# Strided attention in 36-token tiles, loads of k on GpSimd, and weight slots at multiples of 128 bytes, in a sparse attention and MoE kernel

## The chip, the cores and the metric

The kernel runs on one core of one Trainium2 chip. The metric is the device time of one execution in microseconds. The core has five engines with queues of their own: TensorE (PE in the profile; its weight loads are PEld), VectorE (DVE), ScalarE (ACT), GpSimd (POOL) and SyncE (SP), which here issues DMAs. Two on-chip memories are used: a large one in which tiles and weights lie, and eight accumulation banks of 128 x 512 fp32 that PE writes.

## The reference

Attention over 4 batches, 8 heads, 576 tokens and a head dimension of 64, then two feed-forward layers over all 2304 tokens (`_moe_ref` and `_moe2_ref`):

```
rel = pos[:, None] - pos[None, :]
mask_local = (rel >= 0) & (rel < 32)
mask_strided = (rel >= 0) & (pos[None, :] % 32 == pos[:, None] % 32)
# heads 0-3 local, heads 4-7 strided
scores = where(mask, scale * q @ k.T, -1e9)
scores = scores - max(scores)
attn = exp(scores) / (sum(exp(scores)) + 1e-9)
x = (attn @ v)                       # to (2304, 512)
h = x @ w_in                         # w_in 512 x 2048
x = (h * tanh(softplus(h))) @ w_out  # w_out 2048 x 512
h = max(max(x @ w1, x @ w2), x @ w3) # 512 x 768 each
out = h @ w_out2                     # 768 x 512
```

## The kernel before, in words

*Attention.* A head pair is two heads side by side in the 128 partitions. Pairs 0 and 1 of a batch are local, pairs 2 and 3 strided. In a strided head, token t sees only earlier tokens with the same residue t mod 32, of which there are 18. The tokens are taken by residue, 3 residues (54 tokens) to a tile, so that a head has 11 tiles, the last with 2 residues (36 tokens). A unit of work (`unit`, L377) is up to four tiles of a head pair. It computes scores (L413, two matmuls a tile, one per head), on DVE the scaled mask (L426) and the row maximum (L432), on ACT one exponential for each tile with the row's sum accumulated (L438), on DVE guard, reciprocal and normalisation (L445, L448, L451), one PE transpose a tile (L458), on ACT its copy out of the bank (L463), the products with v (L471), and the result's high part on ACT (L489) and low part on DVE (L493). One accumulation bank holds all of a unit, from its scores to its result. Numbers are split into a high and a low part and three partial products are added (`PASSES`), which is why x and the weights have two parts. A plain fp32 matmul (scores, products with v) leaves two records in the trace.

*Loads.* q and k of batch 0 come early in long rows and are transposed by PE (L355). Those of batches 1 to 3 come as four DMAs each for a head pair (`load_qk`, L801), with runs of 32 numbers, and are transposed by DVE (L329). There are two raw buffers for q and two for k. v of a strided pair comes in six DMAs (L834), of a local one in three (L820, L826). All these DMAs and those of the weights (L787, L790) are issued by SP in one order, so a later one stands behind an earlier one that still waits for its buffer.

*Feed-forward layers.* Weights come in 56 pieces of 128 x 512, each as two words a number, and are converted by ACT and DVE (L253 to L281) into slots: 5 of pool a, later 11 of pool x where the attention's buffers were, and 8 of pool y on the right side of the memory where `hr` was. The first four pieces of w_in are applied in blocks of 288 tokens while attention is still running (L516, copied by L526), their products with w_out in blocks of 512 tokens start after it (L543). Then come the other twelve pieces (L516, L543), and the second layer (L590, L615). The last block has 256 tokens.

*Order.* A planner (`Plan`) sets one order for all engines before anything is emitted. It gives every step a cost on its engine, simulates the engines, and always takes the ready step of the lowest rank. Where it expects PE to wait until the first product of L543, it writes matmuls of 256 columns on zeros (`fill`, L839) that take up the expected time. Ring buffers (`RING`) and banks are reused in turn, and a step waits for the last reader of what it writes.

Of the kernel before, what the change touches and what calls it, by code (L numbers as in the profile page):

```python
# [10 lines left out]
F32 = mybir.dt.float32  # L11
# [23 lines left out]
RES = 3  # L35
ATT_BANKS = ("a0", "a1", "a2", "acc1", "acc2")
RAW_BANKS = ("h0", "acc3")
# [152 lines left out]
def build_plan(k, B, H, S, D, DM, FF, FF2, wide):  # L190
# [110 lines left out]
    unit_tiles = {True: ((0, 1, 2), (3, 4, 5), (6, 7, 8)), False: ((0, 1, 2, 3), (4, 5, 6, 7), (8, 9, 10))}  # L301
    per_batch = 3 * H // 2
# [8 lines left out]
    def attention():  # L311
        n = 0
        for i, (b, hp) in enumerate(pairs):
# [7 lines left out]
            for nm in ("q", "k") if b else ():  # L321
                for g in range(4):
                    add("qk_load", "sp", S * PACKET[128], (lambda g=g, nm=nm, b=b, hp=hp, r=r: k.load_qk(nm, g, b, hp, k.raw(nm, r))),
                        writes=[("raw", nm, r, g)], rank=lr)

                def tr(nm=nm, r=r, local=local):
                    t = k.qkT(nm, r)
                    tv = t.rearrange("p (j r) -> p j r", r=STRIDE) if local else t.rearrange("p (r j) -> p j r", j=NJ)
                    nc.vector.transpose(out=tv, in_=k.raw(nm, r))  # L329

                add("tr", "dve", 669, tr, reads=[("raw", nm, r, g) for g in range(4)], writes=[("qT", nm, r)], rank=rk0 - 0.5)
            vparts = k.v_parts(hp)
            for j in range(vparts):
                v_cost = PACKET[256] * (LK * (2 if j == 0 else NL - 1) if local else NJ * (NS - (j % RES == RES - 1)))
                add("v_load", "sp", v_cost, (lambda j=j, b=b, hp=hp, rv=rv: k.load_v(j, b, hp, k.v(rv))),
                    writes=[("v", rv, j_) for j_ in range(j, 2 * RES, vparts)], rank=lr + 0.5)
            for u, tiles in enumerate(unit_tiles[local]):
                unit(n, i, u, tiles, b, hp, local, r, rv)
                n += 1
            if i == H // 2 - 1:  # L340
                add("hrpool", "dve", 0, k.open_hrpool, writes=[("earlypool",)], rank=-1)

    def early_qk(i, b, hp, local, r, rk0, lr):
# [5 lines left out]
        for j in range(2):  # L349
            for nm in ("q", "k"):  # L350
# [9 lines left out]
                def copy(nm=nm, j=j, tag=tag):  # L360
# [3 lines left out]
                    else:  # L364
                        t = t.rearrange("p (r j) -> p r j", j=NJ)[:, :, NJ // 2 * j:NJ // 2 * (j + 1)]
                        src = src.rearrange("p (j r) -> p r j", r=STRIDE)
# [10 lines left out]
    def unit(n, i, u, tiles, b, hp, local, r, rv):  # L377
# [5 lines left out]
        tag = ATT_BANKS[n % len(ATT_BANKS)]  # L383
        bk = ("bank", tag)
# [24 lines left out]
        for j, tl in enumerate(tiles):  # L409
            def scores(j=j, tl=tl):  # L410
                kw = LK if local else width(tl)
                for h in range(2):
                    nc.tensor.matmul(  # L413
                        ps()[LQ * h:LQ * h + width(tl), j * K:j * K + kw],
                        lhsT=cols("q", h, tl), rhs=cols("k", h, tl), start=True, stop=True,
                    )
            add("scores", "pe", 212 if local else 142, scores, reads=[("qT", "q", r), ("qT", "k", r)], writes=[bk], rank=rk, cols=4 * (K if local else width(tl)))

        def mask():
# [4 lines left out]
            else:  # L424
                m = k.m_first[:, 1, :].unsqueeze(1).broadcast_to([rows, nt, K])
            nc.vector.scalar_tensor_tensor(  # L426
                out=sv(), in0=ps()[:rows, :nt * K].rearrange("p (n c) -> p n c", c=K),
# [6 lines left out]
        add("mask", "dve", dve(nt * K), mask, reads=[bk], writes=[sb, *sk], rank=rk)  # L434
# [456 lines left out]
```

## Time and profile before

| | |
|---|---|
| time, three runs | 807.07, 807.09, 807.59 us (median 807.09) |
| the profiled execution | 807.78 us, of it a span of 806.0 us |
| PE busy | 797.0 us (99%), 5017 records |
| DVE busy | 360.7 us (45%) |
| ACT busy | 320.9 us (40%) |
| POOL busy | 4.4 us (1%) |
| PE's granted clock | 1.00 over the whole span |
| share of the span in the chain that ended last | PE 92%, DMA 3%, ACT 2%, DVE 2% |

The span goes from the first to the last instruction of the profiled execution. Busy times of different engines lie beside each other. The chain is followed back from the last instruction, at each step to what released it. The attention with the first blocks of 288 tokens takes the first 154 us or so, and everything after that is matmuls of 512 columns and their small work on DVE and ACT.

### The profile page before, as it was taken

The numbers are of one execution on the slowest core, as the hardware profiler recorded it, in microseconds if no ns is written. First come the engines' busy times: TensorE is split into PE (matmuls) and PEld (weight loads), VectorE is DVE, ScalarE is ACT, GpSimd is POOL, SyncE is SP. The second block draws the span as 40 slices with busy tenths as digits, with TensorE's granted clock in tenths as the row PEclk, the third lists the DMA queues.
The fourth block names the chain that finished last, engine by engine and source line by source line (L and its number), as shares of the span: only waits on it lengthen the run. The fifth ranks groups of instructions, "written<-read, shape, count | busy, mean of one in ns | idle before, by whom it ended". The sixth has DMA issues, their size and how long they took to land.

```text
span 806.0 us, 12605 instructions
## 1 busy us (share of the span) xinstructions
PE 797.0 (99%) x5017; PEld 669.3 (83%) x5017; DVE 360.7 (45%) x769; ACT 320.9 (40%) x839; POOL 4.4 (1%) x22
## 2 busy tenths in 40 slices
PE   9999999999999999999999999999999999999998
PEld 7878888988888888888888899888888888888897
DVE  6988886895931311311321179981212211122222
ACT  5978878997732322312322257630110110110111
POOL 2000000000000000000000000000000000000000
PEclk9999999999999999999999999999999999999999
DMA  9877750944900100100010079200100010010010
GB/s 206 157 152 132 135 102 22 349 148 170 326 0 1 53 0 1 53 0 1 1 52 0 1 227 322 105 1 0 53 1 0 16 38 1 0 53 1 0 53 27
DMA packets 119690, 59.66 MB, mean 74 GB/s; under 512 B 91984, under 2 KB 110416, under 8 KB 119632
## 3 DMA queue, kind: packets, MB, share of 16 engines
q1 hardware_dynamic: 118448, 58.57, 26.5%
q8 instruction: 39, 0.64, 0.3%
q10 hardware_dynamic: 1184, 0.30, 0.2%
q14 instruction: 19, 0.16, 0.1%
HBM read 49.41 MB, written 9.44 MB: 73 GB/s over the span
## 4 chain that ended last, share of the span: by engine, by line
PE 92%; DMA 3%; ACT 2%; DVE 2%; issue 1%; SPq 0%; DVEq 0%; ACTq 0%
PE bank_acc L543 24%; PE bank_a L590 21%; PE bank_a L516 13%; PE bank_acc L615 9%; PE bank_h L516 7%; PE bank_h L590 7%; PE bank_acc L516 3%; PE bank_a L413 2%; PE bank_a L471 1%; DMA wslot<-in_moe_w_dram 1%; PE bank_a L458 1%; DMA wslot<-in_moe_w_out_dram 1%; PE bank_acc L413 1%; ACT s L438 1%; PE bank_acc L471 1%; PE bank_acc L458 1%
## 5 line engine op out<-in xcount | busy, mean ns | idle before, releaser
L543 PE MATMUL bank_acc<-g,wslot 128*128 128x512 f32 (+1 forms) x960 | 205.4, 370 | 1.4 <-ACT g L537 1.0
L543 PEld LDWEIGHTS bank_acc<-g,wslot 128*128 128x128 f32 x960 | 168.3, 188 | 33.7 <-ACT g L537 1.2
L590 PE MATMUL bank_a<-x,wslot 128*128 128x512 f32 (+1 forms) x816 | 174.7, 369 | 0.0
L590 PEld LDWEIGHTS bank_a<-x,wslot 128*128 128x128 f32 x816 | 142.3, 188 | 26.9
L538 DVE TENSOR_TENSOR g<-h,g 128x512 fp32r<-128x512 f32 (+1 forms) x80 | 51.1, 639 | 194.8 <-ACT g L537 194.8
L516 PE MATMUL bank_a<-x,wslot 128*128 128x512 f32 (+1 forms) x540 | 117.2, 369 | 0.0
L516 PEld LDWEIGHTS bank_a<-x,wslot 128*128 128x128 f32 x540 | 94.5, 188 | 17.9
L599 DVE TENSOR_TENSOR h<-bank_a,h 128x512 f32<-128x512 f32 (+1 forms) x46 | 29.2, 635 | 138.9 <-PE bank_a L590 138.9
L615 PE MATMUL bank_acc<-wslot,g 128*128 128x512 f32 x324 | 78.8, 391 | 0.0
L516 PE MATMUL bank_h<-x,wslot 128*128 128x288 f32 (+2 forms) x372 | 74.5, 339 | 0.0
L615 PEld LDWEIGHTS bank_acc<-wslot,g 128*128 128x128 f32 x324 | 60.5, 188 | 12.8
L535 ACT ACTIVATE h<-bank_a 128x512 f32<-128x512 f32 (+1 forms) x45 | 25.0, 555 | 109.8 <-PE bank_a L516 109.8
L516 PEld LDWEIGHTS bank_h<-x,wslot 128*128 128x128 f32 x372 | 58.5, 188 | 7.4
L601 ACT ACTIVATE g<-h 128x512 fp32r<-128x512 f32 (+1 forms) x30 | 17.7, 589 | 116.1 <-DVE h L599 116.1
L590 PE MATMUL bank_h<-x,wslot 128*128 128x512 f32 (+1 forms) x264 | 58.8, 371 | 0.0
L438 ACT ACTIVATE s<-s,st 118x54 f32<-118x54 f32 (+1 forms) x160 | 55.5, 352 | 7.2 <-DVE st L432 6.9
L590 PEld LDWEIGHTS bank_h<-x,wslot 128*128 128x128 f32 x264 | 46.7, 188 | 9.0
L537 ACT CAST g<-h 128x512 fp32r<-128x512 f32 (+1 forms) x80 | 46.3, 579 | 4.5 <-PE bank_acc L543 2.7
L253 ACT ACTIVATE wt<-wslot 128x512 f32<-128x512 f32 x56 | 37.9, 678 | 22.7 <-DVE wslot L281 9.7
L277 ACT CAST wslot<-wt 128x512 fp32r<-128x512 f32 x56 | 34.5, 621 | 15.3 <-DVE wt L267 15.1
L281 DVE TENSOR_TENSOR wslot<-wt,wslot 128x512 fp32r<-128x512 f32 x56 | 38.6, 692 | 3.4 <-ACT wslot L277 3.4
L596 ACT COPY h<-bank_a 128x512 f32<-128x512 f32 (+1 forms) x22 | 12.0, 548 | 69.8 <-PE bank_a L590 69.8
(71 smaller groups left out, 680.4 us busy)
## 6 DMA issues: line engine op xcount, KB each, us to landing
wslot<-in_moe_w_out_dram SPq DMA_DIRECT2D x22, 512.0 KB
wslot<-in_moe_w_dram SPq DMA_DIRECT2D x18, 512.0 KB
wslot<-in_moe_w_in_dram SPq DMA_DIRECT2D x16, 512.0 KB
out_dram<-wt SPq DMA_DIRECT2D x18, 256.0 KB
x2p<-ev SPq DMA_DIRECT2D x16, 256.0 KB
ev<-x2p SPq DMA_DIRECT2D x16, 256.0 KB
rawq<-in_q_dram SPq DMA_DIRECT2D x48, 72.0 KB
rawk<-in_k_dram SPq DMA_DIRECT2D x48, 72.0 KB
```

The lines of the kernel that those rows point to most:

```text
L253: nc.scalar.mul(k.wt(r2).bitcast(F32), k.words(slot)[1].bitcast(F32), 2.0 ** -111)
L277: nc.scalar.copy(out=k.open_slot(slot)[:, 0, :], in_=k.wt(r2).bitcast(F32))
L281: nc.vector.tensor_tensor(out=s[:, 1, :], in0=k.wt(r2).bitcast(F32), in1=s[:, 0, :], op=ALU.subtract)
L438: nc.scalar.activation(sv()[:, j, :], sv()[:, j, :], AF.Exp, bias=mx()[:, j:j + 1], accum_out=dn()[:, j:j + 1],)
L516: nc.tensor.matmul(k.bank(hb)[:, :n], lhsT=wap(("in", f), a, c), rhs=k.x[:, q, c, t0:t0 + n], start=(c == 0 and m == 0), stop=(c == KC - 1 ...
L535: add(name, "act", act(n, psum=not stored), lambda: nc.scalar.activation(Hh(), src(), AF.Mish, scale=W_SCALE), reads=sread, writes=[HK], r ...
L537: add("gh", "act", act(n), lambda: nc.scalar.copy(out=g()[:, 0, :n], in_=Hh()), reads=[HK], writes=[G0], rank=s)
L538: add("gl", "dve", dve(n), lambda: nc.vector.tensor_tensor(out=g()[:, 1, :n], in0=Hh(), in1=g()[:, 0, :n], op=ALU.subtract), reads=[HK, G0 ...
L543: nc.tensor.matmul(k.bank(f"acc{c}")[:, :n], lhsT=wap(("out", f), a, c), rhs=g()[:, q, :n], start=(first and m == 0), stop=(last and m == 2),)
L590: nc.tensor.matmul(k.bank(hb)[:, :n], lhsT=wap((w_, f), a, c), rhs=k.x[:, q, c, t0:t0 + n], start=(c == 0 and m == 0), stop=(c == KC - 1 a ...
L599: add("m2", "dve", dve(n), (lambda hb=hb: nc.vector.tensor_tensor(out=m_(), in0=k.bank(hb)[:, :n], in1=m_(), op=ALU.max)), reads=[("bank", ...
L615: nc.tensor.matmul(k.bank(ab)[:], lhsT=k.g(rg)[:, a, c * P:(c + 1) * P], rhs=t[:, q, :], start=(f == 0 and m == 0), stop=(f == F2C - 1 and ...
```

## The change

- A strided tile has 2 residues (36 tokens), so a head has 16 tiles. They are taken in two units of four steps; a step handles two tiles of a head pair, residues 2n and 2n+1 (tile n) and 16 more than these (tile n + 8; `par` 0 and 1), with both heads: four matmuls of scores of 36 x 36, in two banks, that lie in the four quadrants of 64 x 64 of the array. The products with v do likewise. One PE transpose of 100 x 100 takes two tiles. A new function `pair_unit` emits such a unit; `unit` keeps the local ones.
- Its softmax has one row maximum, one subtraction, one exponential, one sum and one normalisation for eight tiles; the subtraction and the sum are DVE's, the exponential has no bias and no accumulator.
- Local units take one bank for scores (a0, a1 in turn) and another for transposes and results (a2, acc1, acc2 in turn); a strided unit has two for scores and two for the rest.
- Tokens of a strided pair stand in another order inside a tile, and v of a strided pair comes in four DMAs of 36 rows of 2 KB.
- The DMAs of k for batches 1 to 3 are issued by GpSimd. GpSimd also clears the five buffers s (now 128 x 512) at the start, behind the masks.
- The pad `edge` is 24 numbers (96 bytes a partition) in place of 8 (32 bytes). The tiles that lie on the right side behind it, the eight slots of pool y among them, move from 64 past a multiple of 128 bytes to a multiple.

```diff
-RES = 3
+RES = 2
+ATT_PAIRS = (("a0", "a1"), ("a2", "acc1"))
+IN_BANKS, OUT_BANKS = ATT_BANKS[:2], ATT_BANKS[2:]
...
-    unit_tiles = {True: ((0, 1, 2), (3, 4, 5), (6, 7, 8)), False: ((0, 1, 2, 3), (4, 5, 6, 7), (8, 9, 10))}
+    unit_tiles = {True: ((0, 1, 2), (3, 4, 5), (6, 7, 8)), False: ((0, 1, 2, 3), (4, 5, 6, 7))}
...
-                    add("qk_load", "sp", S * PACKET[128], (lambda ...: k.load_qk(nm, g, b, hp, k.raw(nm, r))),
+                    add("qk_load", "sp" if nm == "q" else "qa", S * PACKET[128], (lambda ...: k.load_qk(nm, g, b, hp, k.raw(nm, r))),
...
-        tag = ATT_BANKS[n % len(ATT_BANKS)]
+        tin, tag = IN_BANKS[n % len(IN_BANKS)], OUT_BANKS[n % len(OUT_BANKS)]
...
+    def pair_unit(n, i, u, tiles, b, hp, local, r, rv):
...
+        for j, tl in enumerate(tiles):
+            for par in range(2):
+                def scores(j=j, tl=tl, par=par):
+                    for h in range(2):
+                        o = LQ * (h ^ par)
+                        nc.tensor.matmul(
+                            k.bank(ins[par])[o:o + K, j * K:(j + 1) * K],
+                            lhsT=qk("q", h, NS // 2 * par + tl), rhs=qk("k", h, NS // 2 * par + tl), start=True, stop=True,
+                        )
+                add("scores", "pe", 38, scores, reads=[("qT", "q", r), ("qT", "k", r)], writes=[ik[par]], rank=rk, cols=2 * K)
...
+        add("rowmax", "dve", dve(2 * nt * K), lambda: nc.vector.tensor_reduce(out=mx(), in_=sv(), axis=AX.X, op=ALU.max, negate=True),
+            reads=[sb], writes=[mk], rank=rk)
+        add("sub", "dve", dve(2 * nt * K), lambda: nc.vector.tensor_tensor(out=sv(), in0=sv(), in1=many(mx()), op=ALU.add),
+            reads=[mk], writes=[sb], rank=rk)
+        add("exps", "act", act(2 * nt * K), lambda: nc.scalar.activation(sv(), sv(), AF.Exp), writes=[sb], rank=rk)
+        add("sum", "dve", dve(2 * nt * K), lambda: nc.vector.tensor_reduce(out=dn(), in_=sv(), axis=AX.X, op=ALU.add),
+            reads=[sb], writes=[dk], rank=rk)
...
+                nc.tensor.transpose(
+                    k.bank(outs[0])[:rows, j * P:j * P + rows], k.buf(sb)[:rows, j * P:j * P + rows], k.ident[:rows, :rows]
+                )
...
+                    for h in range(2):
+                        c = j * P + LQ * (h ^ par)
+                        nc.tensor.matmul(
+                            k.bank(outs[par])[D * h:D * (h + 1), j * K:(j + 1) * K],
+                            lhsT=k.v(rv)[o:o + K, h, tl, :], rhs=k.buf(pb)[o:o + K, c:c + K], start=True, stop=True,
+                        )
...
-    upper.tile([P, 8], F32, name="edge")
+    upper.tile([P, 24], F32, name="edge")
...
-        nc.sync.dma_start(
+        (nc.sync if nm == "q" else nc.gpsimd).dma_start(
...
-            h, r = divmod(j, RES)
-            vr = v[b, 2 * hp + h].rearrange("(j r) d -> j r d", r=STRIDE)
-            n = len(range(r, STRIDE, RES))
-            nc.sync.dma_start(out=t[NJ * r:NJ * (r + 1), h, :n, :], in_=vr[:, r::RES, :])
+            h, par = divmod(j, 2)
+            n = NS // 2 * D
+            o = LQ * par
+            nc.sync.dma_start(
+                out=t[o:o + RES * NJ, h, :NS // 2, :].rearrange("p n d -> p (n d)"),
+                in_=v[b, 2 * hp + h].rearrange("(p n) d -> p (n d)", n=NS)[:, n * par:n * (par + 1)],
+            )
...
+        for t in s_t:
+            nc.gpsimd.memset(t[:], 0.0)
```

The lines of the program move by 7 to 104 with it: the fillers L839 become L938, the first layer's L516 and L543 become L612 and L639, the second layer's L590 and L615 become L686 and L711, the loads of q and k L801 become L897, those of strided v L834 become L930.

The planner writes another order for every engine. On PE, batch 0's first strided units stand in these rows before (s is the masked scores, pt their transpose, earlyq and earlyk the early loads, a row ends with its count):

```order
L839 MATMUL bank_acc_105<-x 128x256 x7
L471 MATMUL bank_a_101<-pt_124,v_134 64x64 x6
L458 MATMUL bank_a_102<-ident,s_110 54x118 x4
L839 MATMUL bank_acc_105<-x 128x256 x7
L355 MATMUL bank_h_104<-ident,earlyq_96 128x96 x3
L355 MATMUL bank_acc_108<-ident,earlyk_97 128x96 x3
L458 MATMUL bank_a_103<-ident,s_111 54x118 x4
L839 MATMUL bank_acc_105<-x 128x256 x3
L471 MATMUL bank_a_102<-pt_122,v_135 64x54 x8
```

and now in these (L528 scores, L556 transposes, L569 products with v, L481 the same of a local unit):

```order
L365 MATMUL bank_acc_108<-ident,earlyk_97 128x96 x3
L938 MATMUL bank_acc_105<-x 128x256 x30
L556 MATMUL bank_a_103<-ident,s_110 100x100 x4
L938 MATMUL bank_acc_105<-x 128x256 x5
L365 MATMUL bank_h_104<-ident,earlyq_96 128x96 x3
L569 MATMUL bank_a_103<-pt_122,v_135 64x36 x8
L569 MATMUL bank_acc_106<-pt_122,v_135 64x36 x8
L938 MATMUL bank_acc_105<-x 128x256 x3
L365 MATMUL bank_h_104<-ident,earlyq_96 128x96 x3
```

Between the scores of the first strided unit and its transposes stand fillers in one run of 30, and there are more of them around its products with v; the unit's products go to two banks. Up to the end of batch 0 there are 53 fillers before and 134 now, and over the whole program 61 and 155.

On SP, the loads that follow batch 0's stand in these rows before:

```order
L787 DMA wslot<-in_moe_w_out_dram 128x1024
L801 DMA rawq_125<-in_q_dram 32x18x32 x4
L801 DMA rawk_127<-in_k_dram 32x18x32 x4
L801 DMA rawq_126<-in_q_dram 32x18x32 x4
L801 DMA rawk_128<-in_k_dram 32x18x32 x4
L801 DMA rawq_125<-in_q_dram 32x18x32 x4
L801 DMA rawk_127<-in_k_dram 32x18x32 x3
L834 DMA v_133<-in_v_dram 18x11x64 x2
L834 DMA v_133<-in_v_dram 18x10x64
L834 DMA v_133<-in_v_dram 18x11x64 x2
L834 DMA v_133<-in_v_dram 18x10x64
```

On SP they stand in these now, without k, and with four DMAs for each strided v:

```order
L922 DMA v_134<-in_v_dram 96x8x64 x2
L897 DMA rawq_125<-in_q_dram 32x18x32 x4
L897 DMA rawq_126<-in_q_dram 32x18x32 x4
L897 DMA rawq_125<-in_q_dram 32x18x32 x4
L930 DMA v_133<-in_v_dram 36x512 x4
L897 DMA rawq_126<-in_q_dram 32x18x32 x4
L930 DMA v_134<-in_v_dram 36x512 x4
```

On POOL k's loads now follow the five cleared buffers:

```order
L960 MEMSET s_112 128x512
L960 MEMSET s_113 128x512
L897 DMA rawk_127<-in_k_dram 32x18x32 x4
L897 DMA rawk_128<-in_k_dram 32x18x32 x4
L897 DMA rawk_127<-in_k_dram 32x18x32 x4
```

SP's rows of the whole program go from 182 to 142, the DMAs of k leave between those of q, and POOL has 48 of them.

## Rows read from the trace of the kernel before

**Rows 1.** The page's busy times: busy us (share of the span) x instructions.

```profile
PE 797.0 (99%) x5017; PEld 669.3 (83%) x5017; DVE 360.7 (45%) x769; ACT 320.9 (40%) x839; POOL 4.4 (1%) x22
```

**Rows 2.** Busy us (x instructions) by stretch; then clock, DMA share, GB/s.

```profile
10.00:41.70 31.70, 31.56 (x477) 26.19 (x473) 30.15 (x98) 28.92 (x126) 0.00 (x0) 1.00 0.96 190
41.70:60.00 18.30, 16.60 (x193) 13.21 (x190) 15.81 (x43) 13.00 (x52) 0.00 (x0) 1.00 0.76 141
60.00:100.00 40.00, 40.00 (x579) 33.52 (x579) 34.45 (x107) 32.85 (x145) 0.00 (x0) 1.00 0.74 134
100.00:140.00 40.00, 39.90 (x526) 33.98 (x525) 30.77 (x92) 31.38 (x134) 0.00 (x0) 1.00 0.33 65
...
153.90:460.00 306.10, 306.10 (x1363) 252.32 (x1362) 108.87 (x184) 117.22 (x206) 0.00 (x0) 1.00 0.18 62
```

**Rows 3.** Timeline, 48 to 50 us: start, us, instruction, [idle before, releaser].

```profile
48.04 0.68 ACT L253 ACTIVATE wt<-wslot 128x512 f32<-128x512 f32 x1 [2.32 <-DMA wslot<-in_moe_w_out_dram]
...
49.99 0.53 PE L516 MATMUL bank_acc<-x,wslot 128*128 128x288 f32 x2 [1.00 <-ACT wslot L277]
```

**Rows 4.** Timeline of PE, 143 to 154 us.

```profile
143.40 1.10 PE L839 MATMUL bank_acc<-x 128*128 128x256 f32 x8
144.34 1.74 PE L516 MATMUL bank_h<-x,wslot 128*128 128x288 f32 x12
...
153.91 2.45 PE L543 MATMUL bank_acc<-g,wslot 128*128 128x512 f32 x10
```

**Rows 5.** Timeline of PE, 63 to 72 us, strided units.

```profile
63.17 0.61 PE L413 MATMUL bank_a<-qTk,qTq 64*54 64x54 f32 x16
63.70 0.59 PE L458 MATMUL bank_acc<-ident,s 118*54 118x118 f32 x4
64.06 1.05 PE L516 MATMUL bank_h<-x,wslot 128*128 128x288 f32 x6
...
69.88 0.25 PE L471 MATMUL bank_a<-pt,v 36*64 36x36 f32 x2
69.89 0.26 PE L413 MATMUL bank_acc<-qTk,qTq 64*36 64x36 f32 x2
69.95 0.23 PE L471 MATMUL bank_a<-pt,v 36*64 36x36 f32 x2
...
71.30 0.67 PE L471 MATMUL bank_a<-pt,v 54*64 54x54 f32 x16
71.90 0.67 PE L516 MATMUL bank_acc<-x,wslot 128*128 128x288 f32 x3
```

**Rows 6.** Groups of DVE by shape, 0 to 160 us: busy us, mean ns.

```profile
L432 DVE TENSOR_REDUCE st<-s 128x3 f32<-128x288 f32 x24 | 10.5, 437 | 0.1
...
L432 DVE TENSOR_REDUCE st<-s 118x4 f32<-118x216 f32 x16 | 6.0, 373 | 0.1
...
L493 DVE TENSOR_TENSOR x<-bank_a,x 128x216 fp32r<-128x216 f32 x10 | 5.4, 545 | 3.9 <-ACT x L489 3.7
...
L493 DVE TENSOR_TENSOR x<-bank_a,x 128x144 fp32r<-128x144 f32 x5 | 2.1, 415 | 0.0
```

**Rows 7.** Timeline of SP and DVE, 78 to 86 us.

```profile
78.33 1.23 DVE L329 STREAM_TRANSPOSE qTq<-rawq 128x576 f32<-128x576 f32 x1
...
85.75 2.06 SPq L801 DMA_DIRECT2D rawk<-in_k_dram  x4
...
85.88 1.25 DVE L329 STREAM_TRANSPOSE qTq<-rawq 128x576 f32<-128x576 f32 x1
```

**Rows 8.** Timeline of PE in the second layer, 572 to 603 us.

```profile
572.90 2.88 PE L590 MATMUL bank_a<-x,wslot 128*128 128x512 f32 x12
575.62 0.62 PE L615 MATMUL bank_acc<-wslot,g 128*128 128x512 f32 x2
...
600.10 2.96 PE L590 MATMUL bank_h<-x,wslot 128*128 128x512 f32 x12
602.90 5.76 PE L590 MATMUL bank_a<-x,wslot 128*128 128x512 f32 x24
```

More of the change, by code (lines that the diff above doesn't have):

```diff
@@ L327, in tr @@
                     t = k.qkT(nm, r)
-                    tv = t.rearrange("p (j r) -> p j r", r=STRIDE) if local else t.rearrange("p (r j) -> p j r", j=NJ)
-                    nc.vector.transpose(out=tv, in_=k.raw(nm, r))
+                    src = k.raw(nm, r)
+                    if local:
+                        t = t.rearrange("p (j r) -> p j r", r=STRIDE)
+                    else:
+                        t = in_tile(t, nm).rearrange("p n a j -> p j a n")
+                    nc.vector.transpose(out=t, in_=src)
                 add("tr", "dve", 669, tr, reads=[("raw", nm, r, g) for g in range(4)], writes=[("qT", nm, r)], rank=rk0 - 0.5)
-            vparts = k.v_parts(hp)
+            vparts = 3 if local else 4
             for j in range(vparts):
-                v_cost = PACKET[256] * (LK * (2 if j == 0 else NL - 1) if local else NJ * (NS - (j % RES == RES - 1)))
+                v_cost = PACKET[256] * LK * (2 if j == 0 else NL - 1) if local else 300
                 add("v_load", "sp", v_cost, (lambda j=j, b=b, hp=hp, rv=rv: k.load_v(j, b, hp, k.v(rv))),
-                    writes=[("v", rv, j_) for j_ in range(j, 2 * RES, vparts)], rank=lr + 0.5)
+                    writes=[("v", rv, j_) for j_ in range(j, VKEYS, vparts)], rank=lr + 0.5)
             for u, tiles in enumerate(unit_tiles[local]):
-                unit(n, i, u, tiles, b, hp, local, r, rv)
+                (unit if local else pair_unit)(n, i, u, tiles, b, hp, local, r, rv)
                 n += 1
@@ L413, in scores @@
                     nc.tensor.matmul(
[L414 removed]
+                        k.bank(tin)[LQ * h:LQ * h + width(tl), j * K:j * K + kw],
                         lhsT=cols("q", h, tl), rhs=cols("k", h, tl), start=True, stop=True,
                     )
[L417 removed]
+            add("scores", "pe", 212 if local else 142, scores, reads=[("qT", "q", r), ("qT", "k", r)], writes=[ik], rank=rk, cols=4 * (K if local else width(tl)))
         def mask():
@@ L475, in av @@
                     )
-            add("av", "pe", 160, av, reads=[pk] + [("earlypool",)] * (rv >= RING["v"]) + [("v", rv, j_) for j_ in range(2 * RES)], writes=[bk], rank=rk, cols=8 * width(tl) * K / P)
+            add("av", "pe", 160, av, reads=[pk] + [("earlypool",)] * (rv >= RING["v"]) + [("v", rv, j_) for j_ in range(VKEYS)], writes=[bk], rank=rk, cols=8 * width(tl) * K / P)
         def io(part):
@@ L741, in sparse_attention_moe_kernel @@
     qT_t = {nm: many(atc, "qT", [P, S], suffix=nm) for nm in "qk"}
-    v_t = many(atc, "v", [P, 2, NS, D])
-    v_t += [early_pool.tile([P, 2, NS, D], F32, name=f"v{i}") for i in range(RING["v"], RING["v"] + 2)]
+    v_t = many(atc, "v", [P, 2, NL, D])
+    v_t += [early_pool.tile([P, 2, NL, D], F32, name=f"v{i}") for i in range(RING["v"], RING["v"] + 2)]
     m_first = atc.tile([P, 3, LK], F32, name="m_first")
```

74 lines of the change are left out of this document (64 added, 10 removed).

## The prediction

> **What bounds the kernel now.** I read first the busy time of each engine over the whole span, then the table of stretches, then single rows of the timeline. The first says that TensorE (PE) is busy 99% of 806.0 us [rows 1]: little is to be had from waits, so the time changes by what PE is given to do and by how fast it does it. The table of stretches [rows 2] tells where that is different. In batch 0's attention (10 to 41.7 us) PE is busy 31.56 of 31.70 us, but VectorE (DVE) is busy 30.15 and ScalarE (ACT) 28.92: three engines are full, and part of PE's work is filler. From 41.7 to 60 us PE has 1.70 us of idle time, the largest of the attention; the rows there show it waiting for a converted weight, and ACT waiting for that weight's DMA [rows 3]. From 60 to 140 us PE is full again and DVE is busy 65.2 of 80 us. From 153.91 us, where the first 512-column block of the second matrix starts [rows 4], to 460 us PE is never idle. [...]
>
> So the end follows PE: each microsecond of instructions added to it before 153.9 us moves the end by as much, unless PE stood waiting there, and each matmul made faster later takes as much off.
>
> **The change part by part.**
>
> *Fillers.* The planner writes matmuls of 256 columns where it expects PE to idle. The order of PE holds 61 of them before and 155 after, 94 more, 81 of them in batch 0. Eight of them take 0.94 us from the first's start to the next instruction [rows 4], 0.118 us each: 94 x 0.118 = 11.1 us. They would be free where PE waits anyway, but in batch 0 PE has only 0.14 us of idle time left. Against them stands the strided work that left the same places.
>
> *Strided attention on PE.* Now 88 tiles of up to 54 tokens, afterwards 128 of 36. A fp32 matmul leaves two records, so scores go from 352 to 512 records, and the products with v as well; transposes go from 88 to 64. Now a group of 16 score records takes 0.53 us (63.17 to 63.70), 0.033 each, 4 transposes take 0.36, 0.09 each, and 16 records with v take 0.60, 0.0375 each [rows 5]. Before: 352 x 0.033 + 352 x 0.0375 + 88 x 0.09 = 32.7 us. For the new shape the trace has the 36-wide last tile of a head: in one place two records of products with v and two of scores start within 0.07 us (69.88 to 69.95) [rows 5], 0.018 each. That is with two quadrants of the array in use; the new units go round all four, and if these ran side by side it would be half, 0.009. The cost of going from one kind of matmul to another is what separates 0.033 from the 54-wide pace; scaling 0.018 by 54/36 gives 0.027, and 16 x (0.033 - 0.027) = 0.1 us a group, so I take 0.13 a group for both kinds. After: 16 units of two groups, 32 x 0.13 = 4.2; 64 transposes x 0.09 = 5.8; and 1024 records, 18.4 us at 0.018 or 9.2 at 0.009. Together 28.4 or 19.2: between -4.3 and -13.5 us. On the other side, if four narrow matmuls gain nothing over the 54-wide rates, 512 x 0.033 + 512 x 0.0375 + 5.8 = 41.9, or +9.2. I take 0.016, near the one row of that width, because the two records of a matmul must follow each other in one quadrant: 16.4 + 4.2 + 5.8 = 26.4, **-6.3 us**.
>
> [...] The trace shows four 36-wide records starting 0.018 us apart [rows 5]. [...]
>
> *Softmax.* In place of 88 small exponentials on ACT there are 16 of 288 columns; DVE gets a subtraction and a sum that ACT had done. By DVE's rows [rows 6] a strided head pair costs now three masks, maxima and normalisations (all at the maximum's rate, 373 ns at 216 columns, about 0.32 for the short one) and three low parts (545, 545, 415): 3.2 + 1.5 = 4.7 us. Afterwards it costs four masks of 144 columns (373 less 72 columns at the 0.89 ns by which 288 columns differ from 216: 0.31), eight passes of 288 columns at 0.437 and four low parts at 0.415: 1.2 + 3.5 + 1.7 = 6.4. That is +1.7 us a pair, 3.4 in batch 0 and 10.2 in the other three. I cost it at nothing: in batch 0 the added fillers make PE's side longer by more than DVE's 3.4, and in the later batches DVE has 14.8 us free in 80 [rows 2]. If the cover is gone, it is the third case below.
>
> *Loads.* 48 of the DMAs of k leave SyncE's queue (SP) for GpSimd's, and 16 of the strided v go altogether, as each tile of v comes in 4 DMAs of long rows in place of 6. SP issues four DMAs of k in 2.06 us [rows 7], so its queue is some 48 x 0.5 = 25 us shorter, and the weights that queue behind these loads come earlier. The wait at 48 to 50 us [rows 3] should go. What stands behind it: the idle time of 41.7 to 60 us is 1.70 us in all, so **-1.7 us** at most; I take it whole, with 0 as the other end. GpSimd also clears five buffers of 512 columns at the start. Its 22 instructions take 4.4 us now [rows 1], 0.2 each, so five wider ones may take 1 to 4 us and end before 10 us, where batch 0's softmax starts: nothing, or 2 us if they don't.
>
> *Slots.* The wider pad moves the eight weight slots on the right side of the on-chip memory from 64 past a multiple of 128 bytes to a multiple. The same 12 matmuls of 512 columns take 2.72 us (572.90 to 575.62) with weights in a slot that is at a multiple now, and 2.80 (600.10 to 602.90) from a slot that isn't [rows 8]: 6.67 ns each. Fourteen pieces of weights pass through those slots with 48 such matmuls each, 672 x 6.67 ns = **-4.5 us**. If what differs between these slots is something other than their address, this term is 0.
>
> The sum: 11.1 - 6.3 - 1.7 - 4.5 = -1.4 us. It is made against the profiled execution, 807.78 us with its span of 806.0; the median of the three runs is 807.09, 0.69 below. Taken off the median: **805.7 us**.
>
> **The rivals.**
>
> *Four quadrants side by side.* At 0.009 us a record the strided term is -13.5 and the sum -8.6, 798.5 us; with part of it 802.5. For it: no two of four consecutive matmuls share a quadrant. Against: in the trace only two ever do run together, and two records of one matmul follow each other.
>
> *DVE becomes the bound (slower).* A strided unit's chain now holds nine steps, seven of them on DVE, and in batch 0 DVE is busy 95% of the time. With 10.2 us more in the later batches it would be busy 75.4 of 80 us there. If the transposes then come late, PE waits at each of the 12 later units. Half of the 10.2 on PE's path gives 805.7 + 5.1 = 810.8; all of it 815.9. It decides once DVE passes the 95% that batch 0 shows. Against: the scores of the next unit have banks of their own and can run ahead.
>
> *GpSimd's loads come late (slower).* One tile of k must be issued and land in the time of a head pair; two transposes of q stand 7.55 us apart (78.33 to 85.88) [rows 7], and there are two buffers. How long GpSimd takes over four DMAs of 576 short runs each no row shows; SP's 2.06 us is the lower bound. At 7.55 us nothing is lost, at 9 us each of some 11 tiles falls back by 1.45: +16, 821.7. At 8.2 us it is +7, 812.9.
>
> [...]
>
> [...]
>
> *The slots' addresses don't set the pace.* The change then does not do this part, and the sum is +3.1: 810.2.
>
> **How the numbers follow.** A difference under 0.2% (1.6 us) can't be told from none here, so faster is under 805.5 and slower over 808.7. The forecast, with the strided term between 0.013 and 0.018 us a record and the waits gone or not (802.5 to 808.7), has 0.40, of it 0.22 faster, 0.16 the same and 0.02 slower. Four quadrants side by side have 0.22, all faster. DVE as the bound has 0.13, of it 0.01 the same. GpSimd's loads have 0.11, the floor 0.08, the slots 0.06, all slower. Faster 0.44, same 0.17, slower 0.39. The range reaches from the four quadrants to the middle of the late loads, 799 to 817; the forecast's own is 802.5 to 808.7.
>
> **What would show it.** In the table of stretches after: the first 512-column matmul of the second matrix comes near 153.9 + 11.1 - 6.3 - 1.7 = 157.0 us, batch 0 ends some 6 to 9 us later than 41.7, and the rest from there to the end is 4.5 us shorter. [...] The 12 matmuls of 600.10 us take 2.72. PE's idle time between batch 0 and the first block stays under 1 us; waits for a transpose of k there speak for GpSimd's loads, waits for the strided normalisation for DVE. The forecast is wrong if the first 512-column matmul comes before 152 or after 162 us, or if the rest doesn't shorten.

## The result and the profile after

The changed kernel takes 814.77 us (median of 4 runs, 813.29 to 814.96) against 807.08 us before (4 runs on the same chip), a ratio of 1.0091 with a 95% interval of 1.0074 to 1.0109: slower by 7.7 us. The forecast was 805.7 us. The profiled execution took 814.96 us, its span is 813.2.

The table of stretches answers to [rows 2], with the same columns:

```profile
10.00:41.70 31.70, 31.57 (x476) 27.79 (x474) 28.03 (x84) 20.12 (x69) 4.93 (x9) 0.98 1.08 213
41.70:60.00 18.30, 18.30 (x274) 15.29 (x274) 16.12 (x49) 12.74 (x50) 4.79 (x8) 1.00 0.56 88
60.00:100.00 40.00, 40.00 (x642) 34.75 (x643) 34.92 (x107) 23.53 (x85) 15.03 (x23) 1.00 0.59 126
100.00:140.00 40.00, 40.00 (x618) 33.39 (x617) 32.85 (x101) 23.03 (x78) 5.28 (x8) 1.00 0.32 72
140.00:164.70 24.70, 24.70 (x263) 23.29 (x262) 14.12 (x33) 18.50 (x41) 0.00 (x0) 1.00 0.52 178
```

The 1.70 us of PE's idle time between 41.7 and 60 us are gone: from there PE is busy all the time until the first 512-column matmul. But 34 fillers stand in that stretch now, where one stood, and 91 between 10 and 41.7 us, where 35 stood, so a busy PE does not show that nothing would wait; the experiments on the fillers below tell more. From 10 to 41.7 us DVE is no fuller than before (28.03 us, 30.15 before) and ACT is a third emptier. The clock of 0.98 in the first row is a stretch with a granted clock of 0.50, up to 11.2 us, and 1.00 behind it; the three executions with a mean clock of 1.00 took 813.29 to 814.94 us, so little of the time hangs on it.

The timeline of PE shows what (start, duration, instruction):

```profile
26.98 3.84 PE L938 MATMUL bank_acc<-x 128*128 128x256 f32 x30
30.65 0.51 PE L556 MATMUL bank_a<-ident,s 100*100 100x100 f32 x4
30.94 0.84 PE L938 MATMUL bank_acc<-x 128*128 128x256 f32 x5
...
44.32 0.71 PE L423 MATMUL bank_a<-qTk,qTq 64*64 64x96 f32 x12
44.97 0.38 PE L938 MATMUL bank_acc<-x 128*128 128x256 f32 x1
45.28 0.66 PE L569 MATMUL bank_a<-pt,v 36*64 36x36 f32 x16
45.87 1.70 PE L938 MATMUL bank_acc<-x 128*128 128x256 f32 x12
...
100.25 0.47 PE L528 MATMUL bank_a<-qTk,qTq 64*36 64x36 f32 x16
100.65 0.65 PE L612 MATMUL bank_acc<-x,wslot 128*128 128x288 f32 x3
...
163.71 1.76 PE L612 MATMUL bank_acc<-x,wslot 128*128 128x288 f32 x12
165.31 2.90 PE L639 MATMUL bank_acc<-g,wslot 128*128 128x512 f32 x12
```

Thirty fillers take 3.67 us (26.98 to 30.65), 0.122 each. Sixteen score records of 36 columns take 0.40 us (100.25 to 100.65), where 16 of 54 columns took 0.53 [rows 5]. Four transposes take 0.29, where they took 0.36. But sixteen records of the products with v take 0.59 us (45.28 to 45.87), 0.037 each. That is the 0.60 of the 54-wide ones [rows 5], and there are now 512 of them in place of 352. (The scores of local units at 44.32 us, with 64 weight and 96 moving columns, are used further down.)

The time from each PE record's start to the next, summed by kind up to the first 512-column record of the second matrix (153.91 us before, 165.31 after), gives the whole account. A wait counts with the record ahead of it.

| kind | before, us | after, us | difference |
|---|---|---|---|
| fillers, 61 and 155 | 11.7 | 24.5 | +12.8 |
| strided scores, 352 and 512 records | 12.6 | 11.7 | -0.9 |
| strided products with v, 352 and 512 | 12.2 | 17.3 | +5.1 |
| strided transposes, 88 and 64 | 10.0 | 6.1 | -3.9 |
| all else (local units, early transposes, blocks of 288, start) | 107.3 | 105.6 | -1.7 |
| sum | 153.9 | 165.3 | +11.4 |

From there to the end it takes 647.8 us (813.15 - 165.31), 652.1 before: -4.2. The timeline of the second layer shows 12 matmuls in 2.72 us and 24 in 5.44 also where it had been 2.80 [rows 8]:

```profile
608.82 2.88 PE L686 MATMUL bank_h<-x,wslot 128*128 128x512 f32 x12
611.54 5.60 PE L686 MATMUL bank_a<-x,wslot 128*128 128x512 f32 x24
616.98 2.88 PE L711 MATMUL bank_acc<-wslot,g 128*128 128x512 f32 x12
```

### The profile page after: what moved, and what is told of

Read it like the earlier page. It is cut to its first block, busy times and chain, and to the rows that moved or that the text cites. A ratio compares the mean times of both kernels' runs of the same rounds, so it can differ in the third digit from the quotient of the medians.

```text
span 813.2 us, 13253 instructions
## 1 busy us (share of the span) xinstructions
PE 805.4 (99%) x5407; PEld 683.5 (84%) x5407; DVE 368.3 (45%) x785; ACT 299.5 (37%) x679; POOL 38.5 (5%) x75
## 4 chain that ended last, share of the span: by engine, by line
PE 94%; DMA 3%; DVE 1%; ACT 1%; issue 0%; SPq 0%; ACTq 0%
PE bank_acc L639 22%; PE bank_a L686 21%; PE bank_a L612 12%; PE bank_acc L711 9%; PE bank_h L612 7%; PE bank_h L686 7%; PE bank_acc L612 4%; PE bank_acc L938 2%; PE bank_a L423 2%; PE bank_a L528 1%; DMA wslot<-in_moe_w_dram 1%; DMA wslot<-in_moe_w_in_dram 1%; PE bank_acc L481 1%; PE bank_a L569 1%; PE bank_acc L569 1%; PE bank_acc L468 1%
## 5 line engine op out<-in xcount | busy, mean ns | idle before, releaser
L639 PE MATMUL bank_acc<-g,wslot 128*128 128x512 f32 (+1 forms) x960 | 204.5, 369 | 1.3 <-ACT g L633 0.7
L639 PEld LDWEIGHTS bank_acc<-g,wslot 128*128 128x128 f32 x960 | 168.1, 188 | 33.1 <-DVE g L634 1.5
L686 PE MATMUL bank_a<-x,wslot 128*128 128x512 f32 (+1 forms) x816 | 173.2, 367 | 0.0
L686 PEld LDWEIGHTS bank_a<-x,wslot 128*128 128x128 f32 x816 | 142.4, 189 | 25.5
L612 PE MATMUL bank_a<-x,wslot 128*128 128x512 f32 (+1 forms) x540 | 116.2, 368 | 0.0
L612 PEld LDWEIGHTS bank_a<-x,wslot 128*128 128x128 f32 x540 | 94.7, 189 | 16.8
L711 PE MATMUL bank_acc<-wslot,g 128*128 128x512 f32 x324 | 78.3, 389 | 0.0
L612 PE MATMUL bank_h<-x,wslot 128*128 128x288 f32 (+2 forms) x372 | 75.0, 338 | 0.0
L711 PEld LDWEIGHTS bank_acc<-wslot,g 128*128 128x128 f32 x324 | 60.4, 188 | 12.2
L612 PEld LDWEIGHTS bank_h<-x,wslot 128*128 128x128 f32 x372 | 58.8, 188 | 6.7
L686 PE MATMUL bank_h<-x,wslot 128*128 128x512 f32 (+1 forms) x264 | 58.3, 370 | 0.0
L686 PEld LDWEIGHTS bank_h<-x,wslot 128*128 128x128 f32 x264 | 46.7, 188 | 8.6
L270 DVE SCALAR_TENSOR_TENSOR wt<-wslot,wt 128x512 uint32<-128x512 uint32 x56 | 38.2, 683 | 0.1
L264 DVE SCALAR_TENSOR_TENSOR wt<-wslot,wt 128x512 uint32<-128x512 uint32 x56 | 38.0, 683 | 0.2
```

Of the source, the lines that this page charges most:

```text
L264: nc.vector.scalar_tensor_tensor(out=t, in0=k.words(slot)[1], scalar=0x80000000, in1=t, op0=ALU.bitwise_and, op1=ALU.bitwise_or)
L270: nc.vector.scalar_tensor_tensor(out=t, in0=k.words(slot)[0], scalar=29, in1=t, op0=ALU.logical_shift_right, op1=ALU.bitwise_or)
L612: nc.tensor.matmul(k.bank(hb)[:, :n], lhsT=wap(("in", f), a, c), rhs=k.x[:, q, c, t0:t0 + n], start=(c == 0 and m == 0), stop=(c == KC - 1 ...
L639: nc.tensor.matmul(k.bank(f"acc{c}")[:, :n], lhsT=wap(("out", f), a, c), rhs=g()[:, q, :n], start=(first and m == 0), stop=(last and m == 2),)
L686: nc.tensor.matmul(k.bank(hb)[:, :n], lhsT=wap((w_, f), a, c), rhs=k.x[:, q, c, t0:t0 + n], start=(c == 0 and m == 0), stop=(c == KC - 1 a ...
L711: nc.tensor.matmul(k.bank(ab)[:], lhsT=k.g(rg)[:, a, c * P:(c + 1) * P], rhs=t[:, q, :], start=(f == 0 and m == 0), stop=(f == F2C - 1 and ...
```

## The experiments

All ratios are to the kernel before, run on the same chip with them; its median was between 807.1 and 808.1 us there, so a difference in us between two of these kernels from different chips can be off by about 1 us. "First block" is the start of the first 512-column matmul of the second matrix.

**The place of the slots.** Two kernels, the changed one without this part and the one before with nothing else.

```diff
-    upper.tile([P, 24], F32, name="edge")   # e4, from the changed kernel
+    upper.tile([P, 8], F32, name="edge")
-    upper.tile([P, 8], F32, name="edge")    # e5, from the kernel before
+    upper.tile([P, 24], F32, name="edge")
```

> The changed kernel with the pad of 8 numbers again, so that the eight slots on the right side are at 64 past a multiple of 128 bytes as in the kernel before. Theory A, the place of the slots set the pace of the 512-column matmuls: 3.6 to 4.5 us more, 818.4 to 819.3 us, and 12 matmuls with weights in such a slot take 2.80 us. Theory B, the 3.6 us that the second part of the changed kernel is shorter come from its other order: 814 to 815.5 us.

> The kernel before with the pad of 24 numbers alone. Theory A, the place of the slots is worth by itself what it is worth inside the change: 3.6 to 4.5 us less than before, ratio 0.9945 to 0.9956. Theory B, the gain needs the other order: ratio 0.998 to 1.002.

The first took 819.25 us (1.0144, 1.0125 to 1.0163), 4.5 more than the changed kernel; the second 802.52 (0.9933, 0.9918 to 0.9948), 5.3 less than before. Theory A both times, the second with a gain above its range of 3.6 to 4.5. Behind the first block the second takes 647.9 us, 4.2 less than before, as the changed kernel does. The rows of the first are those of before again, 2.80 and 5.60 us:

```profile
612.10 2.96 PE L686 MATMUL bank_h<-x,wslot 128*128 128x512 f32 x12
614.90 5.76 PE L686 MATMUL bank_a<-x,wslot 128*128 128x512 f32 x24
620.50 2.91 PE L711 MATMUL bank_acc<-wslot,g 128*128 128x512 f32 x12
```

**The products with v.** One kernel loads 36 of the 64 weight columns and leaves the other dimensions of v out, one lets the two row groups (the upper and the lower 64 rows of the array) alternate.

```diff
-    k.bank(outs[par])[D * h:D * (h + 1), ...], lhsT=k.v(rv)[o:o + K, h, tl, :], ...    # e2
+    k.bank(outs[par])[D * h:D * h + K, ...], lhsT=k.v(rv)[o:o + K, h, tl, :K], ...
...
-            for par in range(2):          # e3: one step of four matmuls a tile,
-                def av(j=j, tl=tl, par=par):
-                    for h in range(2):
+            def av(j=j, tl=tl):           # price 76 in place of 2 x 38
+                for h in range(2):
+                    for par in range(2):
```

> The changed kernel, but the strided products with v load 36 of the 64 columns of v as weights, so 28 of the 64 dimensions of a head are left out of these products. Theory A, the 64 weight columns set the pace of these matmuls (16 records in 0.59 us now): 16 records take 0.40 us as the 36-wide scores do, 512 x 0.012 = 6 us less, 808 to 810 us. Theory B, the pace has nothing to do with the weights' width (rows of v, the second bank, or a fixed step): 0.59 us as before, 814 to 815.5 us.

> The changed kernel, with the products with v of one step issued as one piece, alternating between the upper and the lower 64 rows of the array, so that four matmuls in a row lie in four quadrants. Theory A, weights of 64 columns for different row groups load beside each other (in the trace, at 32.23 to 32.42 us where the two banks' products mix, 12 records start in 0.19 us): about 0.016 to 0.02 a record instead of 0.034, 7 to 9 us less, 806 to 808 us. Theory B, the mix at 32.3 us is an accident of how the records end: 0.03 a record or more, 813 to 816 us.

The first took 809.82 us (1.0025, 1.0012 to 1.0037), 5 less than the changed kernel; by the account above its strided products with v take 11.9 us. Its timeline has the sixteen records in 0.40 us, the time of the scores:

```profile
79.47 0.47 PE L569 MATMUL bank_a<-pt,v 36*36 36x36 f32 x16
79.87 1.06 PE L612 MATMUL bank_acc<-x,wslot 128*128 128x288 f32 x6
```

The second took 805.59 us (0.9974, 0.9964 to 0.9984), 9 less than the changed kernel, with all 64 columns. Its 32 records of a unit take 0.60 us (69.43 to 70.03) and start four at a time:

```profile
69.43 0.24 PE L569 MATMUL bank_a<-pt,v 36*64 36x36 f32 x1
69.44 0.24 PE L569 MATMUL bank_acc<-pt,v 36*64 36x36 f32 x1
69.45 0.24 PE L569 MATMUL bank_a<-pt,v 36*64 36x36 f32 x1
69.45 0.24 PE L569 MATMUL bank_acc<-pt,v 36*64 36x36 f32 x1
69.51 0.22 PE L569 MATMUL bank_a<-pt,v 36*64 36x36 f32 x1
...
69.88 0.22 PE L569 MATMUL bank_acc<-pt,v 36*64 36x36 f32 x1
70.03 0.40 PE L612 MATMUL bank_acc<-x,wslot 128*128 128x288 f32 x1
```

Theory A both times; the second is 0.4 us below its range. The strided products with v take 9.7 us by the account above, 17.3 in the changed kernel.

The width of the weights sets the pace in these runs: with 64 columns the records of one `par` (two heads, two quadrants) start in pairs some 0.058 us apart (0.59 us less the 0.13 that the prediction estimated for changing kind, by eight), with 36 columns some 0.034 (0.40 less 0.13, by eight). With both `par` in turn two such streams run beside each other (32 records in the 0.60 us above). The same is seen in the changed kernel where its two runs happen to meet:

```profile
40.45 0.25 PE L569 MATMUL bank_acc<-pt,v 36*64 36x36 f32 x2
40.49 0.23 PE L569 MATMUL bank_a<-pt,v 36*64 36x36 f32 x2
40.52 0.23 PE L569 MATMUL bank_acc<-pt,v 36*64 36x36 f32 x2
40.55 0.23 PE L569 MATMUL bank_a<-pt,v 36*64 36x36 f32 x2
40.58 0.23 PE L569 MATMUL bank_acc<-pt,v 36*64 36x36 f32 x2
```

Different rows are not by themselves what does it. In the scores the two heads of a `par` use different rows already, and sixteen of them take the same 0.40 us as sixteen products with 36 weight columns in the same rows. What pays is that both `par` alternate (32 records in 0.60 us, where 16 of one `par` take 0.59), and with them all four quadrants and two banks; which of the two counts was not tried apart. In the changed kernel the planner put all matmuls of one `par` mostly in a run, those of the scores too, so the quadrants that the layout had made free were seldom used. Alternating the scores was not tried.

**The fillers.** One kernel leaves out all but the first 15, one every second one behind these (with the alternating row groups).

```diff
     def fill():
+        filled[0] += 1
+        if filled[0] > 15:                       # e1, from the changed kernel
+        if filled[0] > 15 and filled[0] % 2:     # e7 from e3, e10 from e5, e11, e12
+            return
         nc.tensor.matmul(banks["acc0"][:, :FILL], ...)
```

> The changed kernel, its order unchanged, with the fillers left out behind the first 15 (140 of 155 are gone; they compute nothing that is used). Theory A, the added fillers are paid for in full on TensorE's path: 140 x 0.12 = 17 us less to do; some of that comes back as waits for DVE in batch 0 (DVE is busy 28.0 of 31.7 us there), so 798 to 804 us, at an unchanged clock. Theory B, the fillers only occupy time in which TensorE would wait: 813 to 816 us, with the idle time of TensorE before 165 us up by some 15 us. Theory C, they hold the clock: a granted clock under 1.0 before 60 us, and a time above 815.

> The version with four quadrants in the products with v, every second filler behind the first 15 left out (77 of 170; nothing used is left out). Theory A, half the fillers hold the clock, and each one gone saves 0.12 us where nothing waits: up to 9 us less, 797 to 803 us, clock 1.00. Theory B, TensorE's clock falls in batch 0 as without fillers (0.65 to 0.69 of 30 to 60 us there): 806 to 815 us.

Without them the changed kernel takes 816.96 us (1.0114, 1.0075 to 1.0153), not 798 to 804. Theory C: the granted clock is 1.00 from 10 to 30 us; then PE stands idle for 3.31 us and waits for the first strided unit's normalisation on DVE, and in the rows that hold this wait and what follows the clock is below it:

```profile
34.41 0.91 PE L556 MATMUL bank_a<-ident,s 100*100 100x100 f32 x4 [3.31 <-DVE s L552]
...
30.00:41.70 11.70, 7.72 (x108) 6.41 (x103) 10.73 (x28) 6.69 (x16) 0.00 (x0) 0.65 0.82 176
41.70:60.00 18.30, 16.15 (x225) 13.31 (x224) 15.56 (x50) 9.85 (x37) 5.28 (x8) 0.69 0.36 71
```

That wait is where the changed kernel has its run of thirty fillers (3.67 us). What the changed kernel would take without its added fillers at a full clock no run shows.

With half of them the kernel with alternating row groups takes 802.48 (0.9943, 0.9922 to 0.9964), 3.1 less than with all, at a clock of 1.00: theory A. The 77 that are gone would have been 9 us by their own time. PE then idles 3.7 us between 10 and 41.7 us and 1.2 up to 60, where it had idled 0.1 in all:

```profile
10.00:41.70 31.70, 28.00 (x459) 23.02 (x459) 28.93 (x88) 20.30 (x69) 6.20 (x10) 1.00 1.07 209
41.70:60.00 18.30, 17.06 (x288) 14.43 (x283) 17.51 (x54) 13.32 (x56) 5.27 (x8) 1.00 0.69 121
```

So about half of that time is a wait that is there anyway, and by the medians only a third of it is saved. The longest of these waits is again for a strided unit's normalisation on DVE (1.07 us, ended at 28.88 us). In the kernel before, with the slots moved, half the fillers save nothing:

> The kernel before with the pad of 24 numbers and every second filler behind the first 15 left out (23 of 61). Theory A, as in the version with four quadrants each filler gone saves a part of its 0.12 us: 1 to 3 us less than the pad alone, 800 to 801.5 us. Theory B, this kernel's fillers stand where TensorE waits, or its clock falls: 802 to 806 us.

It took 803.30 us (0.9944, 0.9924 to 0.9963) against 802.52, theory B: the 23 that are gone are 2.7 us by their own time, and PE's idle time behind 10 us grows by 2.8. There the fillers stood in waits altogether, in the version above in part.

**The planner's prices.** The planner holds 38 ns for two strided matmuls; in the changed kernel, by the rows above, two with v (four records) take 4 x 0.037 us, 148 ns, and two of scores 72. With the row groups alternating, four with v take 8 x 0.018 us, 144 ns.

```diff
-    add("scores", "pe", 38, ...      add("av", "pe", 76, ...
+    add("scores", "pe", 70, ...      add("av", "pe", 140, ...
```

> The version with four quadrants in the products with v, but the planner gets the measured prices: 70 ns for two matmuls of scores (4 records at 0.018) and 140 for four with v (8 at 0.018), in place of 38 and 76. It then writes 149 fillers in place of 170. Theory A, the fillers that were planned for time in which TensorE is really at work go at 0.12 us each and nothing else moves: 2 to 3 us less, 803 us. Theory B, the other order that this gives costs as much: 805 to 808 us.

It took 803.36 us (0.9945, 0.9929 to 0.9962), 2.2 less with 21 fillers fewer: theory A. Every second of the fillers left out as well brings nothing more:

> The version with four quadrants and the measured prices in the planner, every second filler behind the first 15 left out (67 of 149). Theory A, both savings add up (2.2 us for the prices, 3.1 for the fillers): 799 to 801 us. Theory B, the fillers that the right prices leave stand in real waits, so nothing is saved: 802.5 to 804.5 us.

803.33 us (0.9939, 0.9921 to 0.9957): theory B. The 67 that are gone are 7.9 us; PE's idle time behind 10 us grows from 0.3 to 5.7 us, and the profiled execution has a clock of 0.74 from 30 to 41.7 us besides. One without much of that (a mean clock of 0.999 in place of 0.995) took no less, 803.86. With the measured prices, then, the fillers left stand for the most part in waits.

**The loads of k.** Four kernels: the changed one with k planned and issued on SP; the same with the engine alone changed and the order of all else kept; the kernel before with the slots moved and k on GpSimd; and half the fillers with k on SP.

```diff
-    add("qk_load", "sp" if nm == "q" else "qa", ...   # e9, e11; kept in e13
+    add("qk_load", "sp", ...
-    (nc.sync if nm == "q" else nc.gpsimd).dma_start(  # e9, e11, e13; the other way round in e6
+    nc.sync.dma_start(
```

> The changed kernel with the loads of k issued by SP again, all else as changed (its order then has 147 fillers, 155 before). Theory A, GpSimd's loads cost time by the waits and the order that they bring, as with the tiles of 54 tokens, where they took 4 us: 809 to 812 us. Theory B, within the change they cost nothing, because strided v leaves SP's queue shorter: 813 to 816 us.

> The changed kernel with its order kept on TensorE, DVE and ACT, instruction by instruction; only the engine that issues the 48 DMAs of k is SP in place of GpSimd. Theory A, GpSimd's own slowness in issuing costs what the run with k back on SP gained (2.9 us): 811 to 813 us. Theory B, that gain came from the planner's other order with 8 fillers fewer: 814 to 816 us, or more where k now stands behind q on SP.

> The kernel before with the pad of 24 numbers and the 48 DMAs of k for batches 1 to 3 issued by GpSimd; tiles of 54 tokens and v as before. Theory A, GpSimd's loads free SP's queue and TensorE's 1.7 us of waits at 41.7 to 60 us go: 1 to 2 us less than with the pad alone. Theory B, GpSimd's DMAs land later than SP's (it issues one in 0.67 us, and stands 78.6 us in waits) and the transposes of k are late: the same as the pad alone or up to 5 us more.

> The version with four quadrants and half the fillers, the loads of k by SP again. Theory A, GpSimd's loads cost 2 to 4 us here too: 798 to 800.5 us. Theory B, they cost nothing: 801.5 to 804 us.

They took 811.89 us (1.0051, 1.0036 to 1.0066), 815.90 (1.0105, 1.0086 to 1.0124), 806.69 (0.9986, 0.9970 to 1.0003) and 803.12 (0.9937, 0.9919 to 0.9954): theories A, B, B and B. With the order kept, the issuing engine is worth nothing: 815.9 against 814.8. What k on SP gains in the first (2.9 us) comes with another order, in which the first block starts at 161.8 us. What GpSimd costs the kernel before (4.2 us) comes with another order too; its timeline has a wait in it that the kernel with the slots alone doesn't have. ACT's copy, for which PE waits, stands behind a conversion that waits for a weight, not for k; the granted clock of the stretch that holds this wait, 41.7 to 60 us, is 0.91 in the mean, and twelve records of 288 columns behind the wait take 2.58 us, 1.60 at 163.71 us above:

```profile
44.27 0.66 ACT L253 ACTIVATE wt<-wslot 128x512 f32<-128x512 f32 x1 [2.36 <-DMA wslot<-in_moe_w_out_dram]
45.35 0.57 PE L471 MATMUL bank_a<-pt,v 96*64 96x64 f32 x12 [2.86 <-ACT pt L463]
...
47.67 2.64 PE L516 MATMUL bank_h<-x,wslot 128*128 128x288 f32 x12
50.25 0.57 PE L471 MATMUL bank_acc<-pt,v 96*64 96x64 f32 x12
...
41.70:60.00 18.30, 15.44 (x164) 12.69 (x163) 14.30 (x37) 11.30 (x43) 3.88 (x7) 0.91 0.60 107
```

Four DMAs of k take GpSimd 2.64 us to issue. In the changed kernel GpSimd stands idle before them until DVE has gone on, and among DVE's waits between 10 and 165 us there is none for a load of k, so nothing waited for these loads:

```profile
90.46 2.65 POOL L897 DMA_DIRECT2D rawk<-in_k_dram  x4 [4.72 <-DVE st L442]
```

Whether the order or GpSimd's start made the kernel before slower in that run was not tried with its order kept, and stays open.

**All together.** Alternating row groups, the measured prices, k on SP. In the first three runs below the planner put the mask of a strided unit ahead of transposes of the local unit that had used the same buffer: three in the first two runs, two in the third. Those transposes took wrong data, so these three kernels compute something else than the reference, and their times stand for nothing but their order. The rule missing in the changed kernel's planner is that the mask overwrites the parts of the buffer under the names that local units give them:

```diff
-    add("mask", ..., reads=[ik[par]], writes=[sb], rank=rk)
+    add("mask", ..., reads=[ik[par]], writes=[sb, *((*sb, j_) for j_ in range(4))], rank=rk)   # and the same for st
```

> Four quadrants in the products with v, the measured prices in the planner, and k on SP: the planner writes 106 fillers in place of 149. Theory A, fillers are what the order costs: 43 fewer at 0.12 us, of which a part comes back as waits: 798 to 801 us. Theory B, the fillers that went stood in waits, and batch 0 ends when its DVE and ACT are done: 802 to 805 us.

> The version with four quadrants, the measured prices and k on SP once more, unchanged, on whatever chip it gets. Theory A, its 799.0 us is what this order takes: 797 to 801 us. Theory B, that run was a disturbed one: 802 to 805 us.

> As the version with four quadrants, measured prices and k on SP, but 150 in place of 140 as the price of four matmuls with v: another order, with 101 fillers in place of 106. Theory A, fewer fillers set the time: 798 to 801 us. Theory B, the single order counts, and 799 us was a lucky one: 801 to 805 us.

> As the version with four quadrants, prices of 70 and 150 and k on SP, but the planner is told all that a strided unit's mask overwrites: in the orders of the two runs before, it put the mask of a strided unit ahead of three transposes (two in the second) of the local unit that used the same buffer five units earlier, so those transposes took wrong data and the output wasn't the reference's. The new order has 104 fillers. Theory A, the time came from the fillers and not from that misplaced mask: 798 to 801.5 us. Theory B, the misplaced mask is what made it fast: 802 to 805 us.

> The same with prices of 72 and 146, 103 fillers, another order again. Theory A: 798 to 801.5 us; theory B: 802 to 805 us. If the two differ by over 2 us, a single order counts for more than the number of fillers.

The first three took 798.97, 798.76 and 800.64 us, each inside its theory A, but as they compute something else this decides nothing. With the rule mended, the times are 802.12 (0.9940, 0.9921 to 0.9959) with prices of 70 and 150, just inside theory B, and 800.12 (0.9909, 0.9895 to 0.9924) with 72 and 146, inside theory A. The last is the fastest version that computes everything, 7 us under the kernel before; 5.3 of that the slots alone give. The two differ by 2.0 us with nearly the same number of fillers (104 and 103), but their intervals overlap and the runs of the first reach from 799.4 to 806.3 us. So neither theory is shown, and that a single order is worth as much as 2 us is likely, not shown.

## Why the prediction was wrong

The time lies inside the whole range of 799 to 817 us, in a part that stood for rivals whose reasons did not come as described. The forecast itself failed at one term.

- *What bounds the kernel* was right in part. PE is busy up to the first block, and the sign of being wrong that the prediction had named came there: the block starts at 165.3 us, after 162. But part of what fills PE is filler over waits. DVE's softmax of a strided unit was costed at nothing because the added fillers make PE's side longer than DVE's; the planner writes them just where it expects PE to wait, and the runs with fewer fillers show waits for DVE in those places (3.31 and 1.07 us). So *DVE becomes the bound* did not come as a wait in the changed kernel, and stands in part behind its fillers. *GpSimd's late loads* did not come: the run with k's engine alone changed shows no gain.
- *Strided attention on PE* is the step that failed. It gave -6.3 us; by the account it is +0.3 (-0.9, +5.1, -3.9). The products with v are 17.3 us where the working has 10.3 (512 x 0.016 and half of 4.2), and that is more than the term's whole miss of 6.6: the scores are 11.7 for 10.3, the transposes 6.1 for 5.8, and the three together had been put 2.2 too low for the kernel before (34.9 for 32.7). A run of scores came as the trace had shown the width (0.40 us for 16 records, the 0.018 and 0.13 of the working give 0.42). That the two records of a matmul must follow each other in one quadrant, the reason for 0.016, no run shows by itself; less the 0.13, the runs showed 0.017 a record for the scores and 0.029 for the products with v. The products with v were given the same 0.016 from one place where two records of them and two of scores mixed [rows 5], and the row that stood beside it, 16 records with v in 0.60 us against 0.53 for the scores of the same width, should have warned: 0.0375 was no matter of the 54 moving columns but of the 64 weight columns, which the change does not narrow. The run with 36 weight columns shows it. With the step put right by alternating the row groups, the term is -7.9 us (27.0 for 34.9) and the time 805.59, next to the forecast of 805.7; there are 170 fillers in that version, so the nearness is in part luck.
- *Fillers* take about what was forecast of PE's time, 12.8 us for 11.1. What was missed is, first, that the price is not what they cost, since part of them stands in waits (above), and second, that some are there because the prices in the code were too low for the very matmuls that then ran long (2.2 us by experiment). The prediction took fillers and strided work for independent terms; with a price too low they come together.
- *The waits*: all else is 1.7 us shorter, for 1.7. The reason given is not shown. ACT's wait for a weight's DMA [rows 3] is not in the trace after, but it is not in the run with k on SP in the same order either, so it did not go because k had left SP's queue; whether the fewer loads of v, the order or the fillers took it away was not tried.
- *The slots* were right: -4.5 forecast, 4.2 in the profile, 4.5 and 5.3 by experiment.
- *The floor*, with its chance of 0.08: no run shows a least step between the starts of narrow matmuls. In the changed kernel 32 records of scores take 0.57 us (91.20 to 91.77), 0.018 each, and with rows alternating four records start within 0.02 us (69.43 to 69.45). *Four quadrants side by side* was right about the array, as those four starts show, and wrong about the order, in which the quadrants came two at a time.
- The forecast's own range has a slip: at 0.018 us a record and with the waits not gone its terms give 807.1 + 11.1 - 4.3 - 4.5 = 809.4, not 808.7.

The sum with the measured terms: fillers +12.8, strided +0.3, all else -1.7, slots -4.2 makes +7.2, and the two profiled executions differ by 814.96 - 807.78 = 7.2.

## What to carry to other kernels

Price a narrow matmul from a row of the same form, with both its weight and its moving columns: here 64 weight columns took the same time with 36 moving columns as with 54 (0.59 and 0.60 us for 16), and the local units' scores with 64 weight and 96 moving columns took longer still (0.65 us for 12). Let neighbours go round all four quadrants (9 us here). Where a planner writes filler work, a price that is too low also buys filler (2.2 us here), so measure the prices of a new shape before the order is judged. A full engine with filler on it does not say that nothing waits; take half of the filler out and see how much of it comes back as idle time. And try the place of the weights in memory by itself: here 16 floats of padding were worth more than all the rest (5.3 of 7 us).

## What the runs showed of the hardware

- Twelve fp32r matmuls of 512 columns took 2.80 us (233.3 ns each) with weights that start at 64 past a multiple of 128 bytes, and 2.72 (226.7) with weights at a multiple.
- Fp32 records with weights of 64 columns started 0.029 us apart within one `par` (0.59 us for 16, less the estimated 0.13 for changing kind), those with 36 columns 0.017 (0.40 us for 16, less the same); with both `par` alternating, 64 columns went at 0.015 (0.60 us for 32, less the same).
- GpSimd took 2.64 us to issue four DMAs of 576 short runs, SP 2.06 [rows 7]; in the same order it made no difference (815.9 us with SP, 814.8 with GpSimd).
